# Attention and mixture of experts in one kernel: the first slot's split divided over two attention units, and the weights' scales taken with their first split

## The chip, the cores and the metric

One core of one Trainium2 chip. The metric is the device time in microseconds of one execution. The kernel before takes 730.81 us (median of 3 runs, 727.73 to 730.84).

## What is computed

For 8 batches of 8 heads, 576 positions and 64 channels, attention is computed twice: on queries, keys and values pooled by four, and locally, within three positions to either side. The sum is the input of a mixture of 8 experts with one expert per token.

```python
out_d = sm_attn(q_d, k_d, v_d)                       # pooled by 4
out_up = np.repeat(out_d, factor, axis=2)
mask = np.abs(pos[:, None] - pos[None, :]) < factor
out_local = np.matmul(attn, v)                       # softmax under the mask
x = (out_up + out_local) -> [N=4608, 512]
...
logits = xn @ en.T / tau
expert_idx = np.argmax(logits, axis=1)
for e in range(E):
    h = np.maximum(x[mask] @ w1[e], 0.0)             # 512 -> 1024
    out[mask] = gate_w[mask, None] * (h @ w2[e])     # 1024 -> 512
```

## The kernel before

**Attention.** There are 32 units: 8 batches of four head pairs. `attention` (a generator) runs a software pipeline over `i` from −2 to 32. In one iteration unit `i+2` has its queries and keys transposed (`qk_T`, PE L378; four ACT copies to `kq`, L379) and pooled on POOL (L392, and the values' `pool_v` L401); unit `i+1` its scores (L407, L412, pooled L434), maxima and exponentials (DVE L423 and L424, L443; ACT L425, L454), row sums, `inv`, and the normalised weights `an` (L472) and `ad` (L477) on DVE; unit `i` the transposes of its weights (PE L485 and L496; ACT copies `aT` L488 and `adT` L498) and the products with the values (L505, L521; ACT `od` L511, DVE `xT` L523); unit `i-1` the transposes to rows of `x` and the experts' logits (L536, L539; ACT `xr` L543, DVE L546; `ls` L548 and L550). The order of instructions on every engine is that in which the program writes them, and each engine runs its own in order; seven PSUM banks go round among the matmuls' results.

**What is placed between.** The generator stops at marks, and the caller puts other work there: `yield i, 0` in the middle of an iteration, `yield i, 3` in front of the rows' copies in iteration 30, `yield i, 1` at the end.

```python
for at in steps:
    if at is None:
        break
    if at in EARLY:
        next(early)
    i, end = at
    if end and i >= 1 and i % NHP in heavy:
        heavy = next(w0, ())
```

`early_slots` makes the lists of the first three expert slots from the tokens that are already there: `ege` and `efull`, then `parts` (L694), which PE multiplies (L702), then the ids (L706 to L732) and on POOL three gathers by them from `xd` in DRAM (L1126), then slot 0's measure (`x_size`: ACT's square L1144, DVE's logits and scale L1145, L79 to L81) and its split into two halves of 16 bits (`x_split`: ACT L1153, DVE L1156, and a transpose by DMA, L1158), then slot 1's. `first_weights` prepares the first expert's weights in four pieces each of `w1` and `w2`: squares and sums on ACT (L859), a total over the partitions with a matmul (L868), the scale `wscl` from it on DVE (L869 to L878), then for each piece the high half on ACT (`w1h`, `w2h`, L882) and the low half on DVE (L887), put off until behind unit `i+1`'s pooled maxima. What a step yields says at which `i % 4` the next may come: `FREE` at any, `LIGHT` at 0, 2, 3, `HEAVY` at 0, 3. Its last two steps issue the loads of the second expert's `w1`, four of 512 KB on SP's queue. When the attention's loop is over, the slots follow, 41 in all, with the matmuls of L1205 to L1207 (`x` by `w1`) and L1228 to L1230 (by `w2`), each product in three parts of 16-bit halves. `warm_up(n)` issues n matmuls of 512 columns whose result nobody reads (L337).

Of the kernel before, what the change touches and what calls it, by code (L numbers as in the profile page):

```python
# [9 lines left out]
F16 = mybir.dt.float16  # L10
BF16 = mybir.dt.bfloat16
I32 = mybir.dt.int32
AF = mybir.ActivationFunctionType
ALU = mybir.AluOpType
# [6 lines left out]
N, DM, E, FF = B * S, H * D, 8, 1024  # L21
# [20 lines left out]
LW = TB + TR  # L42
XS, HS, EB = 3, 10, 127
FIRST = 3
EARLY = ((28, 0), (28, 1), (29, 0), (30, 3), (31, 0), (31, 1))
MASKED = -1.0e30
QS = 0.125 / 16

# [3 lines left out]
class Kern:  # L52
# [128 lines left out]
    def attention(self, ctx):  # L181
# [56 lines left out]
        for i in range(-2, n + 1):  # L238
            a, c, d, e = i + 2, i + 1, i, i - 1
            if a < n:  # L240
                st[a] = {"u": a, "j": a % 2, "vw": self.vw[a // 2 % 2], **half[a // 2]}
                self.qk_T(st[a])
            if a == n:
                self.warm_up(2)
            if 0 <= c < n:
                self.scores(st[c])
                if not c:
                    self.warm_up(3)
            if a < n:
                self.pooled(st[a])  # L250
                for u in range(a if a > 1 else 0, a + 1 if a else 0):
                    self.pooled_v(st[u])
                if a % 2:
                    load_v(a // 2 + 1)
            if i in (0, 2):
                next(clists)
            if 0 <= d < n:
                self.weights_T(st[d])
            if 0 <= c < n:
                self.scores_d(st[c])  # L260
                self.exps(st[c])
                self.peaks_d(st[c])
                while self.later:
                    self.later.pop(0)()
                if c == n - 1:
                    self.exps_d(st[c])
            if 0 <= d < n:
                self.weights_dT(st[d])
                if not d:
                    self.warm_up(7)  # L270
            if 0 <= c < n - 1:
                self.exps_d(st[c])
            yield i, 0
            if mid:
                mid.pop()()
            for _ in range(2 if BEARLY * NHP <= i < (BEARLY + 1) * NHP else 1):
                if tail and i < n - 1:
                    tail.pop(0)()
            self.shared, parts = self.bank(), None
            if 0 <= e < n:  # L280
                b, hp = units[e]
                if hp == 0:
                    xr[b] = (self.rt.tile([TB, NTB, XW], F32, name="xr", bufs=2),
                             self.rt.tile([128, LP], F32, name="ls")[:, :LW])
                parts = self.rows(st.pop(e), hp, *xr[b])
            if 0 <= d < n:
                self.values_d(st[d])
            if c == n - 1:
                self.sums_l(st[c])
                self.inverses(st[c])  # L290
                self.normalise_l(st[c])
                self.normalise_d(st[c])
                yield i, 3
            if 0 <= c < n - 1:
                self.sums_l(st[c])
            if parts:
                parts[1]()
            if 0 <= d < n:
                self.out_d(st[d])
            if 0 <= c < n - 1:  # L300
                self.inverses(st[c])
                self.normalise_l(st[c])
            if 0 <= d < n:
                self.values(st[d])
            if parts:
                parts[0]()
                if hp == NHP - 1:
                    while tail and b >= BEARLY:
                        tail.pop(0)()
                    tail += self.place(b, *xr.pop(b), mid)  # L310
                    if b == B - 2:
                        tail.pop(0)()
            if 0 <= c < n - 1:
                self.normalise_d(st[c])
            if i == n - 1:
                tail.pop(0)()
            if i == -1:
                next(crows)
                nc.vector.memset(self.lg, 0.5)
                nc.vector.memset(self.oh, 0.0)  # L320
            if a >= 0 and a % 2 == 1:
                load(a // 2 + 2)
                if a == 1:
                    load_w(1)
            if d >= 0 and d % 2 == 1:
                load_w(d // 2 + 2)
            yield i, 1
# [384 lines left out]
    def early_slots(self):  # L712

        nc, v = self.nc, self.nc.vector
        c = self.cp
        self.ids = c.tile([128, NEARLY + NSLOT], I32, name="ids")
        full = c.tile([128, 1], F32, name="efull")
        lim = c.tile([128, NEARLY], F32, name="elim")
        for i in range(NEARLY):
            v.memset(lim[:, i:i + 1], float(SLOT * (i + 1)))  # L720
        ge = c.tile([128, NEARLY], F32, name="ege")

        v.tensor_scalar(out=ge, in0=lim, scalar1=self.base[:, 0:1], scalar2=None, op0=ALU.is_le)
        v.reduce_sum(out=full[:, 0:1], in_=ge, axis=AX.X)
        v.tensor_scalar(out=ge, in0=ge, scalar1=-float(PADID), scalar2=float(PADID), op0=ALU.mult, op1=ALU.add)
        self.nearly = full[:, 0:1]
        yield
        parts = self.id_parts(c, self.pb[:, :BEARLY].rearrange("p b t -> p (b t)"), BEARLY, NEARLY)
        yield
        idf = c.tile([128, NEARLY], F32, name="idf")  # L730
        self.ids_of(c, parts, BEARLY * NTB, NEARLY, idf)
        v.tensor_tensor(out=self.ids[:, :NEARLY], in0=idf, in1=ge, op=ALU.max)  # L732
        for q in range(NEARLY):
            self.gather(q)
        yield
        self.x_size(0)
        self.norms(0)
        self.x_split(0)
        yield
        self.x_size(1)  # L740
        yield
        self.x_split(1)
        self.begun = [self.mm1_half(0, 0, 0, 2)]
        yield
# [155 lines left out]
    def first_weights(self):  # L900
# [35 lines left out]
        square(0, 0, 1)  # L936
        yield LIGHT
        square(0, 2, 3)
        yield FREE
        self.total(slice(0, 1))  # L940
        self.scales(slice(0, 1))
        self.keep_scale()
        yield HEAVY
        split(0, 0)
        yield HEAVY
        split(0, 1)
# [5 lines left out]
        square(1, 0, 1)  # L952
        yield LIGHT
        square(1, 2, 3)
        yield FREE
        self.total(slice(1, 2))
        self.scales(slice(1, 2))
        yield HEAVY
        split(1, 0)
        yield HEAVY  # L960
        split(1, 1)
# [1 line left out]
        split(1, 2)  # L963
        yield HEAVY
        split(1, 3)
        self.out_scale()
        for i in range(2):
            yield FREE
            for j in range(2):
# [165 lines left out]
        self.x_split(q, other)  # L1135

    def x_size(self, q):
        nc, s = self.nc, self.sl[q]
        xg = s["xg"]
        v = nc.vector  # L1140
        ss = s["ss"] = self.mx.tile([SLOT, 1], F32, name="ss", bufs=4)
        sc = s["sc"] = self.mx.tile([SLOT, 1], F32, name="sc", bufs=4)
        lg = s["lg"] = self.mx.tile([SLOT, E], F32, name="lg", bufs=4)
        nc.scalar.activation(out=self.jk[:, :DM], in_=xg[:, :DM], func=AF.Square, accum_out=ss)  # L1144
        v.tensor_copy(out=lg, in_=xg[:, DM:])  # L1145
        self.pow2(self.mx, ss, sc)

    def x_split(self, q, other=None):
        nc, s = self.nc, self.sl[q]
        xs = s.pop("xg")[:, :DM]  # L1150
        v, sc = nc.vector, s["sc"]
        x2 = self.mx.tile([SLOT, 2, DM], F16, name="x2")
        nc.scalar.activation(out=x2[:, 0], in_=xs, func=AF.Copy, scale=sc)  # L1153
        if other is not None:
            self.logits(other)
        v.scalar_tensor_tensor(out=x2[:, 1], in0=xs, scalar=sc, in1=x2[:, 0], op0=ALU.mult, op1=ALU.subtract)  # L1156
        xT = s["xT"] = self.mx.tile([128, 2, self.KC, SLOT], F16, name="xT2", bufs=3)
        nc.sync.dma_start_transpose(out=xT.rearrange("p t c s -> p (t c) s"), in_=x2.rearrange("p a f -> p (a f)"))  # L1158

# [86 lines left out]
    def run(self):  # L1246
# [9 lines left out]
        with ExitStack() as actx:  # L1256
            w0 = self.first_weights()
            steps = self.attention(actx)
            early, heavy = self.early_slots(), FREE
# [3 lines that stand above are left out]
                if at in EARLY:  # L1263
                    next(early)
                i, end = at
                if end and i >= 1 and i % NHP in heavy:
                    heavy = next(w0, ())

            ps = self.begun
            self.x_size(2)  # L1270
            self.mm1_half(0, 0, 2, 3, ps[0])
            next(steps)
            self.mm1_half(0, 0, 3, 4, ps[0])
            ps.append(self.mm1_half(0, 1, 0, 2))
            next(steps)
            next(steps)
            for _ in steps:
                pass
# [96 lines left out]
```

## Time and profile before

| | |
|---|---|
| median of 3 runs | 730.81 us (727.73 to 730.84) |
| the profiled execution | 730.06 us, span 728.1 us |
| mean granted clock of TensorE, share of full | 0.983 |
| PE busy | 698.2 us, 96% |
| DVE, ACT, POOL busy | 464.4, 466.7, 403.7 us |
| DMA | 117.82 MB, mean 162 GB/s |

Times of rows are microseconds from the span's start. The duration of a merged row (x4) runs from the first instruction's start to the last one's end; idle time stands in brackets, with what was seen to end it. Attention takes the first 270 us or so of the span, the slots the rest. Unit `i`'s transposes (L485) begin at 87.90 for `i` = 9 and at 262.56 for `i` = 31, the last.

### The profile page before, as it was taken

Reading aid. Unit: us, or ns where it says so; the run is one execution under the profiler, and the core shown is the slowest. Engines: PE = TensorE matmul, PEld = TensorE weight load, DVE = VectorE, ACT = ScalarE, POOL = GpSimd, SP = SyncE. Lnnn points to the kernel's source line nnn. Section 1 sums busy time; section 2 is a strip of 40 time slices with the busy share of each in tenths; the row PEclk is TensorE's granted clock in tenths of the full one; section 3 lists DMA queues with packets and bytes.
Section 4 is the critical chain, followed back from the end, with each engine's and each line's share of the span. In section 5 each row is a group of like instructions: output and inputs, shape, how many; then the busy total and the mean of one; then the engine's idle time right before and its main releaser. Section 6 shows DMA issues by size and latency. Waiting matters only on the chain. (4 is left out here: it accounts for less than half of the span.)

```text
span 728.1 us, 27458 instructions
## 1 busy us (share of the span) xinstructions
PE 698.2 (96%) x10501; PEld 527.0 (72%) x10501; DVE 464.4 (64%) x1395; ACT 466.7 (64%) x1095; POOL 403.7 (55%) x800
## 2 busy tenths in 40 slices
PE   8998999999999989999999999999999999999993
PEld 5787787787878667677767767766776776777671
DVE  6777788797898958757446466564754375456420
ACT  4787877888877654556746658576673367357520
POOL 8554646765776916547543554556465535535421
PEclk9999999999999879999999999999999999999997
DMA  8999887999968357344826566386673346348300
GB/s 192 196 239 255 177 225 161 257 246 196 236 154 226 86 185 212 89 101 165 184 78 200 167 185 187 103 242 113 181 171 87 90 165 177 90 126 214 60 31 20
DMA packets 191238, 117.82 MB, mean 162 GB/s; under 512 B 162898, under 2 KB 162898, under 8 KB 191072
## 3 DMA queue, kind: packets, MB, share of 16 engines
q1 hardware_dynamic: 183264, 94.61, 53.1%
q0 software_dynamic: 6560, 19.03, 8.4%
q10 hardware_dynamic: 1248, 2.11, 1.0%
q8 instruction: 85, 1.39, 0.8%
q14 instruction: 81, 0.66, 0.3%
HBM read 213.12 MB, written 20.33 MB: 321 GB/s over the span
## 5 line engine op out<-in xcount | busy, mean ns | idle before, releaser
L1207 PE MATMUL bank<-xT,w1l 128*128 128x128 f16 x1312 | 223.3, 219 | 2.9 <-DVE w1l L887 1.4
L1206 PE MATMUL bank<-xT,w1h 128*128 128x128 f16 x1312 | 223.5, 219 | 0.4 <-issue 0.3
L1205 PE MATMUL bank<-xT,w1h 128*128 128x128 f16 x1312 | 223.6, 219 | 0.0
L1205 PEld LDWEIGHTS <-w1h 128*128 128x128 f16 x1312 | 128.6, 98 | 7.0 <-issue 2.4
L1207 PEld LDWEIGHTS <-w1l 128*128 128x128 f16 x1312 | 128.6, 98 | 5.0 <-DVE w1l L887 2.6
L1206 PEld LDWEIGHTS <-w1h 128*128 128x128 f16 x1312 | 128.6, 98 | 4.1 <-issue 0.5
L1230 PE MATMUL bank<-w2h,hT 128*128 128x512 f16 x328 | 124.3, 379 | 0.0
L1229 PE MATMUL bank<-w2l,hT 128*128 128x512 f16 x328 | 124.2, 379 | 0.0
L1228 PE MATMUL bank<-w2h,hT 128*128 128x512 f16 x328 | 124.2, 379 | 0.0
L1242 POOL DMA_INDIRECT out_dram<-o,ids x40 | 51.0, 1274 | 111.8 <-ACTq L1042 74.3
L1217 DVE SCALAR_TENSOR_TENSOR hT<-bank,hT 128x512 f16<-128x512 f32 x82 | 54.9, 686 | 44.3 <-ACT hT L1216 19.7
L1216 ACT ACTIVATE hT<-bank 128x512 f16<-128x512 f32 x82 | 46.6, 587 | 51.0 <-PE bank L868 33.1
L392 POOL TENSOR_TENSOR pool_kq<-kq 128x288 f32<-128x288 f32 x62 | 40.2, 670 | 56.4 <-ACT kq L379 54.7
L1156 DVE SCALAR_TENSOR_TENSOR x<-xg,sc,x 128x512 f16<-128x512 f32 x41 | 30.8, 751 | 60.1 <-ACT x L1153 52.9
L859 ACT ACTIVATE junk<-st 128x1024 bf16<-128x1024 f32 (+1 forms) x30 | 67.5, 2248 | 2.1 <-POOL at L618 1.6
L1126 POOL DMA_INDIRECT xg<-xd,ids x41 | 44.4, 1083 | 38.7 <-POOLq L1048 17.2
L401 POOL TENSOR_TENSOR pool_v<-ld_v 72x256 f32<-72x256 f32 x64 | 54.6, 873 | 18.7 <-DMA ld_v<-in_v_dram 17.1
L1230 PEld LDWEIGHTS <-hT 128*128 128x128 f16 x328 | 32.0, 98 | 38.7
L1228 PEld LDWEIGHTS <-hT 128*128 128x128 f16 x328 | 32.0, 98 | 33.8
L1229 PEld LDWEIGHTS <-hT 128*128 128x128 f16 x328 | 32.0, 98 | 33.8
L1174 ACT ACTIVATE lg<-lg,lmx 128x8 f32<-128x8 f32 x41 | 12.3, 300 | 66.8 <-DVE lmx L1172 65.6
L488 ACT ACTIVATE aT<-bank 70x384 f32<-70x384 f32 x96 | 40.1, 486 | 20.9 <-PE bank L485 20.8
(238 smaller groups left out, 1519.3 us busy)
## 6 DMA issues: line engine op xcount, KB each, us to landing
st<-in_moe_w_dram SPq DMA_DIRECT2D x148, 1024.0 KB
ld_k<-in_k_dram SPq DMA_DIRECT2D x64, 144.0 KB
ld_q<-in_q_dram SPq DMA_DIRECT2D x64, 144.0 KB
ld_v<-in_v_dram SPq DMA_DIRECT2D x16, 576.0 KB
vw<-in_v_dram SPq DMA_DIRECT2D x16, 576.0 KB
xd<-xr SPq DMA_DIRECT2D x8, 1040.0 KB
st<-in_moe_w_dram SPq DMA_DIRECT2D x12, 512.0 KB
st<-in_moe_w_dram ACTq DMA_DIRECT2D x4, 512.0 KB
```

What stands on the lines that cost most here:

```text
L401: g.tensor_tensor(out=t6[:, h], in0=vr[:, :, 0:2 * D], in1=vr[:, :, 2 * D:], op=ALU.add)
L859: self.nc.scalar.activation(out=junk, in_=src, func=AF.Square, accum_out=acc)
L1126: nc.gpsimd.indirect_dma_start(out=xg, out_offset=None, in_=self.xd[:n], in_offset=bass.IndirectOffsetOnAxis(ap=self.ids[:, q:q + 1], axis=0),
L1205: nc.tensor.matmul(out=o, lhsT=self.w1h[:, k, f], rhs=xT[:, 0, k], start=(k == 0), stop=False)
L1206: nc.tensor.matmul(out=o, lhsT=self.w1h[:, k, f], rhs=xT[:, 1, k], start=False, stop=False)
L1207: nc.tensor.matmul(out=o, lhsT=self.w1l[:, k, f], rhs=xT[:, 0, k], start=False, stop=(k == self.KC - 1))
L1216: nc.scalar.activation(out=h[:, 0], in_=ps, func=AF.Relu)
L1217: nc.vector.scalar_tensor_tensor(out=h[:, 1], in0=ps, scalar=0.0, in1=h[:, 0], op0=ALU.max, op1=ALU.subtract)
L1228: nc.tensor.matmul(out=ps, lhsT=hh, rhs=self.w2h[:, j, :], start=(j == 0), stop=False)
L1229: nc.tensor.matmul(out=ps, lhsT=hh, rhs=self.w2l[:, j, :], start=False, stop=False)
L1230: nc.tensor.matmul(out=ps, lhsT=hl, rhs=self.w2h[:, j, :], start=False, stop=(j == self.FC - 1))
L1242: nc.gpsimd.indirect_dma_start(out=self.out, out_offset=bass.IndirectOffsetOnAxis(ap=self.ids[:, q:q + 1], axis=0), in_=o, in_offset=None, ...
```

## The change

The table `EARLY`, which says at which marks `early_slots` goes on, has nine entries instead of six. The first (`ege`) moves from iteration 28 to 27 and `parts` to the middle of iteration 28. Slot 0's measure and split are cut into four steps: the square at a new mark `(30, 4)`, ahead of `weights_T`; logits and scale at a new mark `(30, 5)`, behind unit 31's maxima and exponentials; the high half at `(30, 0)`; the low half and the transpose at `(30, 3)`, which moves from in front of the rows' copies to behind unit 30's values. The two warm-up matmuls of iteration 30 go. In `first_weights`, total and scales come in the same step as the first split, for `w1` and for `w2`, and the outputs' scale with the latter; such a step, now `HEAVY`, comes where the split alone came an iteration or more later.

```diff
-EARLY = ((28, 0), (28, 1), (29, 0), (30, 3), (31, 0), (31, 1))
+EARLY = ((27, 0), (28, 0), (29, 0), (30, 4), (30, 5), (30, 0), (30, 3), (31, 0), (31, 1))
...
-            if a == n:
-                self.warm_up(2)
             if 0 <= c < n:
                 self.scores(st[c])
...
+            if c == n - 1:
+                yield i, 4
             if 0 <= d < n:
                 self.weights_T(st[d])
             if 0 <= c < n:
                 self.scores_d(st[c])
                 self.exps(st[c])
+                if c == n - 1:
+                    yield i, 5
                 self.peaks_d(st[c])
...
                 self.normalise_d(st[c])
-                yield i, 3
...
             if 0 <= c < n - 1:
                 self.normalise_d(st[c])
+            if c == n - 1:
+                yield i, 3
...
-        self.x_size(0)
+        self.x_square(0)
+        yield
+        self.x_scale(0)
         self.norms(0)
-        self.x_split(0)
+        yield
+        self.x_high(0)
+        yield
+        self.x_low(0)
         yield
...
-        yield FREE
+        yield HEAVY
         self.total(slice(0, 1))
         self.scales(slice(0, 1))
         self.keep_scale()
-        yield HEAVY
         split(0, 0)
...
-        yield FREE
+        yield HEAVY
         self.total(slice(1, 2))
         self.scales(slice(1, 2))
-        yield HEAVY
+        self.out_scale()
         split(1, 0)
...
         split(1, 3)
-        self.out_scale()
...
     def x_size(self, q):
+        self.x_square(q)
+        self.x_scale(q)
...
     def x_split(self, q, other=None):
...
+        self.x_high(q)
         if other is not None:
             self.logits(other)
...
+        self.x_low(q)
...
-                if end and i >= 1 and i % NHP in heavy:
+                if end == 1 and i >= 1 and i % NHP in heavy:
                     heavy = next(w0, ())
```

`x_square`, `x_scale`, `x_high` and `x_low` hold the lines that `x_size` and `x_split` held: the square into `ss`; the copy of the logits `lg` and the scale `sc`; ACT's copy with that scale; DVE's rest and the transpose.

The weights' steps come so: `w1`'s splits at the end of iterations 8, 11, 12, 15 (before: 11, 12, 15, 16), the squares of `w2` in 16 and 18 (18, 19), its total in 19 (20), its splits in 19, 20, 23, 24 (23, 24, 27, 28). On SP's queue the first load of a `w2` piece moves ahead of the second store of `xd`, and the four loads of the second expert's `w1` stand together ahead of the last `ld_v`; before, two stood behind the store of `xd` in iteration 29 and two behind slot 0's transpose. POOL's order is unchanged. In the rows that follow, the lines of the changed program are some 3 to 19 higher.

ACT at the end of iteration 8 and the start of iteration 9, before (`kq_111` and `kq_107` are the two buffers of `kq`, `st_749` is the staged weights):

```order
L511 ACTIVATE od<-bank 128x144
L543 ACTIVATE xr<-bank 128x4x128
L379 ACTIVATE kq_111<-bank 128x288 x4
L488 ACTIVATE aT<-bank 70x384 x3
L425 ACTIVATE a<-a 128x342
L498 ACTIVATE adT<-bank 72x288 x2
L454 ACTIVATE ad,sums_110<-bank,md 72x144 x4
```

and now:

```order
L514 ACTIVATE od<-bank 128x144
L546 ACTIVATE xr<-bank 128x4x128
L890 ACTIVATE w1h<-st_749,wscl 128x2x512
L382 ACTIVATE kq_111<-bank 128x288 x4
L491 ACTIVATE aT<-bank 70x384 x3
L428 ACTIVATE a<-a 128x342
L501 ACTIVATE adT<-bank 72x288 x2
L457 ACTIVATE ad,sums_110<-bank,md 72x144 x4
```

The split `w1h`, which waits for `wscl`, stands between `xr` and the copies of `kq`; it stood there in iteration 11 before.

ACT from the end of iteration 29 to the end of iteration 30, before (`junk,ss<-xg` is slot 0's square, `x_6006` its high half):

```order
L511 ACTIVATE od<-bank 128x144
L543 ACTIVATE xr<-bank 128x4x128
L488 ACTIVATE aT<-bank 70x384 x3
L425 ACTIVATE a<-a 128x342
L454 ACTIVATE ad,sums_114<-bank,md 72x144 x4
L498 ACTIVATE adT<-bank 72x288 x2
L1144 ACTIVATE junk,ss<-xg 128x512
L1153 ACTIVATE x_6006<-xg,sc 128x512
L511 ACTIVATE od<-bank 128x144
L543 ACTIVATE xr<-bank 128x4x128
```

and now:

```order
L514 ACTIVATE od<-bank 128x144
L546 ACTIVATE xr<-bank 128x4x128
L1151 ACTIVATE junk,ss<-xg 128x512
L491 ACTIVATE aT<-bank 70x384 x3
L428 ACTIVATE a<-a 128x342
L457 ACTIVATE ad,sums_114<-bank,md 72x144 x4
L501 ACTIVATE adT<-bank 72x288 x2
L1169 ACTIVATE x_5984<-xg,sc 128x512
L514 ACTIVATE od<-bank 128x144
L546 ACTIVATE xr<-bank 128x4x128
```

The square moved from behind unit 30's `adT`, where the high half stood too, to ahead of unit 30's `aT`; the high half stayed.

DVE in iteration 30, before (`sc` and `pw_h` are the scale's steps, `x_6006<-xg,sc` the low half of slot 0, `ls` the last rows' copy):

```order
L465 RECIPROCAL inv<-inv 128x13
L472 TENSOR_TENSOR an_113<-a,inv 64x9x38 x2
L477 TENSOR_TENSOR ad<-ad,inv 72x576
L1145 COPY lg<-xg 128x8
L79 TENSOR_SCALAR pw_h<-ss 128x1
L80 TENSOR_SCALAR pw_h<-pw_h 128x1
L81 TENSOR_SCALAR sc<-pw_h 128x1
L1156 SCALAR_TENSOR_TENSOR x_6006<-xg,sc,x_6006 128x512
L546 COPY xr<-bank 128x128
L548 TENSOR_TENSOR ls<-ls,bank 128x192
L523 TENSOR_TENSOR xT_108<-bank,od 128x320
L523 TENSOR_TENSOR xT_108<-bank,od 128x256
```

and now:

```order
L81 TENSOR_SCALAR sc<-pw_h 128x1
L446 TENSOR_REDUCE md<-bank 72x2 x2
L462 TENSOR_REDUCE sums_114<-a 128x9
L467 TENSOR_SCALAR inv<-sums_114 128x13
L468 RECIPROCAL inv<-inv 128x13
L475 TENSOR_TENSOR an_113<-a,inv 64x9x38 x2
L480 TENSOR_TENSOR ad<-ad,inv 72x576
L549 COPY xr<-bank 128x128
L551 TENSOR_TENSOR ls<-ls,bank 128x192
L526 TENSOR_TENSOR xT_108<-bank,od 128x320
L526 TENSOR_TENSOR xT_108<-bank,od 128x256
L1174 SCALAR_TENSOR_TENSOR x_5984<-xg,sc,x_5984 128x512
```

The scale moved ahead of `md`, the maxima of unit 31, and the low half from ahead of `xr` and `ls` to behind `xT`.

## Rows read from the trace of the kernel before

**Rows 1.** The page's first part: busy us (share) and instructions of engines.

```profile
PE 698.2 (96%) x10501; PEld 527.0 (72%) x10501; DVE 464.4 (64%) x1395; ACT 466.7 (64%) x1095; POOL 403.7 (55%) x800
```

**Rows 2.** PE's timeline, 244–275 us: start, duration, instruction, count, [idle before <-releaser].

```profile
247.76 0.90 PE L702 MATMUL bank<-parts,at 128*128 128x6 bf16 x30 [0.94 <-DVE a L424]
...
256.58 1.18 PE L485 MATMUL bank<-ident,an 128*70 128x128 f32 x9
...
260.82 0.76 PE L505 MATMUL bank<-adT,vd 72*64 72x144 f32 x8 [0.71 <-ACT adT L498]
...
265.78 0.98 PE L496 MATMUL bank<-ident,ad 72*72 72x72 f32 x8 [2.05 <-ACT od L511]
...
271.78 0.27 PE L1205 MATMUL bank<-xT,w1h 128*128 128x128 f16 x1
```

**Rows 3.** Windows: length, busy PE PEld DVE ACT POOL, clock, DMA share, GB/s.

```profile
136.00:144.00 8.00, 7.99 (x176) 6.48 (x175) 5.56 (x14) 7.02 (x22) 7.76 (x13) 1.00 0.97 217
218.00:223.00 5.00, 4.43 (x91) 3.42 (x93) 3.87 (x10) 3.25 (x9) 3.25 (x5) 0.66 1.03 331
249.60:256.50 6.90, 6.63 (x128) 4.76 (x127) 6.06 (x24) 1.50 (x7) 4.61 (x5) 0.51 0.67 210
266.70:273.60 6.90, 6.90 (x82) 5.84 (x81) 3.20 (x16) 3.23 (x9) 0.12 (x1) 0.51 0.57 176
```

**Rows 4.** Instructions of tile w1h: ns min/median/max, first and last start.

```profile
L882 ACT ACTIVATE w1h<-st,wscl x32: 1131/1134/1151, 108.5 to 648.2; 128x1024 f16<-128x1024 f32 x32
```

**Rows 5.** ACT's timeline, 84–93 us: copies of kq at iteration 8's end.

```profile
85.65 1.32 ACT L379 ACTIVATE kq<-bank 128x288 f32<-128x288 f32 x4
```

**Rows 6.** DVE's timeline in 84–93 us: ad and the scale of the weights.

```profile
87.08 0.74 DVE L477 TENSOR_TENSOR ad<-ad,inv 72x576 f32<-72x576 f32 x1
...
88.18 0.14 DVE L878 TENSOR_SCALAR wscl<-wk 128x1 int32<-128x1 int32 x1
```

**Rows 7.** PE's timeline in 84–93 us: the transposes of unit 9's weights.

```profile
87.90 1.18 PE L485 MATMUL bank<-ident,an 128*70 128x128 f32 x9
```

**Rows 8.** DVE's timeline in 171–181 us: ad in iteration 19.

```profile
172.56 0.74 DVE L477 TENSOR_TENSOR ad<-ad,inv 72x576 f32<-72x576 f32 x1
```

**Rows 9.** PE's timeline in 169–183 us: L485 beside squares, and a wait.

```profile
172.75 1.51 PE L485 MATMUL bank<-ident,an 128*70 128x128 f32 x9
...
180.25 0.30 PE L407 MATMUL bank<-mask,identb 128*128 128x342 bf16 x1 [0.46 <-DVE xT L523]
```

**Rows 10.** DVE's timeline in 240–268 us.

```profile
248.35 1.27 DVE L887 SCALAR_TENSOR_TENSOR w2l<-st,wscl,w2h 128x1024 f16<-128x1024 f32 x1
...
253.38 1.03 DVE L472 TENSOR_TENSOR an<-a,inv 64x342 f32<-64x342 f32 x2
...
264.11 0.75 DVE L1156 SCALAR_TENSOR_TENSOR x<-xg,sc,x 128x512 f16<-128x512 f32 x1 [0.79 <-ACT x L1153]
```

**Rows 11.** POOL's timeline in 228–268 us.

```profile
230.31 1.42 POOL L401 TENSOR_TENSOR pool_v<-ld_v 72x256 f32<-72x256 f32 x2
...
247.26 2.95 POOL L401 TENSOR_TENSOR pool_v<-ld_v 72x256 f32<-72x256 f32 x2
...
251.31 1.27 POOL L1126 DMA_INDIRECT xg<-xd,ids  x1 [0.30 <-DVE lmx L588]
```

**Rows 12.** DMA queues, 255–257 us: packets, MB, share; q0 is the gathers'.

```profile
q0 software_dynamic: 75, 0.26, 39.1%
```

**Rows 13.** ACT's timeline in 242–268 us.

```profile
257.20 1.24 ACT L488 ACTIVATE aT<-bank 70x384 f32<-70x384 f32 x3 [3.33 <-PE bank L485]
...
260.94 0.64 ACT L1144 ACTIVATE junk<-xg 128x512 bf16<-128x512 f32 x1
```

**Rows 14.** DMA queues in 266.5–267.5 us.

```profile
q1 hardware_dynamic: 810, 0.20, 106.4%
```

**Rows 15.** Timeline of SP's queue in 228–268 us.

```profile
231.76 0.30 SPq L354 DMA_DIRECT2D ld_v<-in_v_dram  x1
```

**Rows 16.** PE's timeline in 131–138 us: a gap in iteration 15.

```profile
136.01 0.27 PE L485 MATMUL bank<-ident,an 128*70 128x128 f32 x1 [1.19 <-issue]
```

More of the change, by code (lines that the diff above doesn't have):

```diff
@@ L1137, in x_size, with x_square, x_scale, x_high @@
     def x_size(self, q):
+        self.x_square(q)
+        self.x_scale(q)
+    def x_square(self, q):
         nc, s = self.nc, self.sl[q]
         xg = s["xg"]
-        v = nc.vector
         ss = s["ss"] = self.mx.tile([SLOT, 1], F32, name="ss", bufs=4)
+        nc.scalar.activation(out=self.jk[:, :DM], in_=xg[:, :DM], func=AF.Square, accum_out=ss)
+    def x_scale(self, q):
+        s = self.sl[q]
         sc = s["sc"] = self.mx.tile([SLOT, 1], F32, name="sc", bufs=4)
         lg = s["lg"] = self.mx.tile([SLOT, E], F32, name="lg", bufs=4)
-        nc.scalar.activation(out=self.jk[:, :DM], in_=xg[:, :DM], func=AF.Square, accum_out=ss)
-        v.tensor_copy(out=lg, in_=xg[:, DM:])
-        self.pow2(self.mx, ss, sc)
+        self.nc.vector.tensor_copy(out=lg, in_=s["xg"][:, DM:])
+        self.pow2(self.mx, s["ss"], sc)
     def x_split(self, q, other=None):
[L1149 to L1153, printed above, removed]
+        self.x_high(q)
         if other is not None:
             self.logits(other)
-        v.scalar_tensor_tensor(out=x2[:, 1], in0=xs, scalar=sc, in1=x2[:, 0], op0=ALU.mult, op1=ALU.subtract)
+        self.x_low(q)
+    def x_high(self, q):
+        s = self.sl[q]
+        x2 = s["x2"] = self.mx.tile([SLOT, 2, DM], F16, name="x2")
+        self.nc.scalar.activation(out=x2[:, 0], in_=s["xg"][:, :DM], func=AF.Copy, scale=s["sc"])
+    def x_low(self, q):
+        nc, s = self.nc, self.sl[q]
+        xs, x2 = s.pop("xg")[:, :DM], s.pop("x2")
+        nc.vector.scalar_tensor_tensor(out=x2[:, 1], in0=xs, scalar=s["sc"], in1=x2[:, 0], op0=ALU.mult,
+                                       op1=ALU.subtract)
         xT = s["xT"] = self.mx.tile([128, 2, self.KC, SLOT], F16, name="xT2", bufs=3)
```

## Prediction, made before the changed kernel ran

> **What bounds the kernel now.** I first read the page's busy times: TensorE (PE) works for 96% of the span [rows 1], so a change is worth what it does to PE's start times and to its clock. Next I followed PE's timeline, attention unit by attention unit, looking for idle time in brackets, and for what the engine named there was doing. The hand-over from attention to the expert slots is where it shows: L702 starts after 0.94 us of idle time, L505 waits 0.71 us, L496 waits 2.05 us, and only at 271.78 does the first slot's first matmul (L1205) start [rows 2]. Last I read the windows for the granted clock: 0.51 in 249.6–256.5 and in 266.7–273.6, 0.66 over 218–223, against 1.00 in 136–144 [rows 3]. [...] A stretch of 6.9 us costs up to half of it, 3.4, where PE is what the others wait for; the one in 218–223 costs (1 − 0.66) × 5 = 1.7.
>
> **The early weights: a loss.** Total, scales and split of the first piece now come in one step. At the end of iteration 8 ScalarE (ACT) gets `w1h`, 1.13 us [rows 4], directly ahead of the four `kq` copies that began at 85.65 [rows 5]. It needs `wscl`, which VectorE (DVE) makes only behind `ad`: done at 88.18 + 0.14 = 88.32 [rows 6]. So ACT stands still with `kq` queued behind it: `w1h` from 88.37, `kq` from about 89.45, 3.8 us later. `kq` empties PSUM banks that the transposes of L485 need: six of the nine, which began at 87.90 [rows 7], run until about 88.65, and the last three wait for the first `kq` copy, done near 89.45 + 0.35 = 89.8. PE idles 1.2 us, and with the copies behind I take **+1.3** (bounds: 0.6, if one more bank is free, and 2.4, if the later copies hold PE up too).
>
> Iteration 19 is the same with `w2h`. `ad` starts at 172.56 [rows 8]; in iteration 8 it started at 87.08, 1.24 us before `wscl` was done [rows 6], so `wscl` comes at 173.80 and `kq` near 174.9. L485 there began at 172.75, took 1.51 us and ended at 174.26 [rows 9]; now its last third waits for 174.9 + 0.35 and ends near 175.6, 1.35 later, with one idle piece of some 1.8 us in it. Part comes back, because PE then waited 0.46 us for DVE at 180.25 [rows 9] and DVE need not be late: **+0.9** (0.5 to 1.4). In iteration 16 two squares stand where a split stood; L485 beside squares took 1.51, beside none 1.18 [rows 7, 9]: **+0.3** (0 to 0.5). The other steps of the weights trade a split for a split, or a square for a square: nothing, the same work stands in the same place of another unit. The first `w2` piece, loaded earlier, puts 512 KB ahead of loads on SP's queue; those are issued a pair of units before they are used, which hides it: nothing, at most 1.5 us (512 KB at the 331 GB/s of rows 3) if not. Together **+2.5** (1.1 to 4.3).
>
> **The late part: a gain.** The splits `w2l` and `w2h` leave iterations 28 and 29 (as the loop counts where DVE does them), and the lists of slot 0 move ahead. Three things follow.
>
> First, `parts` are made ahead of unit 30's row sums, so L702 doesn't wait for them: about 246.7 instead of 247.76. With 1.27 us of `w2l` at 248.35 [rows 10] gone from between, DVE reaches the ids some 1.9 us sooner (1.1 from L702, the rest until L702's result is the later one), and so also `an`, at 251.5 instead of 253.38 [rows 10]. L485 of unit 30, at 256.58 before [rows 2] at the end of a stretch at half clock and of two warm-ups, now starts as soon as `an` is there: near 252.5.
>
> Second, GpSimd (POOL): two `pool_v` took 2.95 us at 247.26, beside `w2l`, and 1.42 at 230.31, without it [rows 11]. With 1.5 us less there, the first gather starts near 249.7 instead of 251.31 [rows 11]. Its 0.26 MB passed in 255 to 257 [rows 12], so it had landed by 257.0, 5.7 us after its start. I keep 5.4, since two weight loads no longer share that time: 255.1. ACT's square (0.64 and a small read, 0.85 together) now stands ahead of `aT` of unit 30, so this landing counts: `aT` at 256.0 against 257.20 [rows 13]. L505, 3.6 us behind `aT` as before, comes near 259.5 instead of 260.82 [rows 2]. Between 252.5 and 259.5 PE waits some 4 us in pieces: a new wait, of ACT for the gather, takes the place of lost clock.
>
> Third, the split of slot 0. DVE did the scale and the low half `x`, 0.75 us at 264.11 [rows 10], ahead of `ls`; ACT's `od` waited for `ls`, and L496 for `od`, 2.05 us [rows 2]. Now the scale is made before unit 31's peaks, ACT's high half follows `adT`, and the low half stands behind `xT`. With all of it 1.35 us sooner, the 1.5 us of scale, wait and `x` out of the way, L496 starts near 263.0 instead of 265.78. From there to L1205 it was 6.0 us, 5.1 of it at the 0.51 of rows 3; at full clock 0.9 + 2.6 and some weight loads, I take 4.1: L1205 at 267.1. The low half is done near 264.1, and its transpose moved its packets until 267.5 [rows 14], 2.6 us behind the end of `x`: 266.7. That is just in time, and it is what is late next if DVE slips.
>
> L1205 at 271.78 was followed by 1.8 us at half clock, which cost 0.9, so it stood like 272.65: 5.5 us gained at full clock. I take off 0.5 for one short stretch at half clock in iteration 30, where PE waits anyway: **−5.0**. Bounds: −6.5 (gather at its soonest), −2.1 (6.9 us at half clock from 263 on, 3.4 off).
>
> Four loads of 512 KB go ahead of the `ld_v` issued at 231.76 [rows 15]. At 331 GB/s they take 6.3 us; the tile comes near 239.5 to 240, about when `pool_v` of unit 30 wants it. If it is late, POOL's list work and the gathers, which are queued behind, are late by as much; cover is the 1.5 us that `pool_v` saves. Nothing, up to 1.5.
>
> Sum: +2.5 − 5.0 = **−2.5** against the profiled execution's 730.06, which is 0.75 under the median of 730.81. Against the median: **728.3**.
>
> [...] The gather's packets passed only in 255 to 257 [rows 12], four microseconds after its start, while SP's queue had a store and two loads to move. [...] By the row the gather lands at 255.1, as summed. [...]
>
> **The rivals.**
> 1. [...] Chance 0.15.
> 2. *The clock stays up.* The loss in 218–223 may not return once all before it is shifted by 2.5 us (1.7), nor any in iteration 30 (0.5): −4.7, **726.1**. Against it: the waits in the late part are shorter, not gone. Chance 0.13.
> 3. *The gather lands no sooner*, at 257.0, so the change doesn't bring what it is moved for. Square, `aT` and what follows are 1.9 later than I count, though the split is still out of DVE's way before `ls`: late gain 2.5 to 3, sum about 0, **730.8**. Chance 0.20.
> 4. *The clock falls at the new waits*, the slower side. Place: PE's idle pieces of 1.2 us in iteration 8 and 1.8 in iteration 19. Price: 3.4 each, by the 249.6–256.5 row, which followed a gap of just 0.94; 1.7 each by the 218–223 row. It decides once both fall for long: −2.5 + 6.8 = +4.3, **735.1**; both short, +0.9, 731.7. Against it: the 1.19 us gap at 136.01 [rows 16] was followed by 1.00 [rows 3]. Chance 0.13.
>
> The forecast keeps 0.39.
>
> **How the numbers follow.** About 0.5%, 3.65 us, is what a measurement of this kernel can tell from no change, so 727.2 to 734.5 counts as the same. Rivals 1 and 2 lie below, by 0.5 and 1 us, so most of their 0.28 counts, 0.20, and the forecast with its lower bounds gives 0.10: faster 0.30. Rival 4 with long stretches, 0.07, and the upper bounds of the third and of the early terms, 0.05: slower 0.12. The rest, 0.58, is the same. The range goes from rival 2 less 1.1 (the early terms nearer to their lower bound), 725.0, to 733.5: rival 3 with the early terms at 4.3 is 732.6, and rival 4 with one short and one long stretch 733.4.
>
> **What would show it.** Right: ACT idle before `w1h` at 88 and before `w2h` at 174, with L485 broken in two there; no idle time at L702; gather 0 near 249.7; the square ahead of `aT` at 255; L496 near 263; L1205 near 267. Wrong: PE not idle in iterations 8 and 19 (no early loss: 725.8); a stretch below 1.00 behind either; the gather's packets not before 257; L1205 waiting for the transpose and not for PE, which would say that DVE ends the hand-over.

## The result, and the profile after

The changed kernel takes 737.26 us (median of 13 runs, 731.69 to 740.93); the kernel before, in 13 runs beside them, 730.81. The ratio is 1.0083 with an interval of 1.0055 to 1.0112: about 6 us slower, outside the range of the prediction (725.0 to 733.5) and on the other side. The profiled execution took 734.77, its span is 732.8. All ratios leave out the executions that lie over 1.5% above the fastest of their kernel.

The page's first part, the counterpart of [rows 1]: PE works no longer than before, so the time went into waits.

```profile
PE 696.9 (95%) x10499; PEld 525.7 (72%) x10499; DVE 464.0 (63%) x1395; ACT 466.5 (64%) x1095; POOL 402.4 (55%) x800
```

Windows of the clock, as in [rows 3]: one stretch of 3.4 us near 200 and one of 13.6 in the hand-over; at the first slot's first matmul, 277.24, the clock is full again (1.00 in 276–280).

```profile
199.00:204.00 5.00, 5.00 (x102) 4.05 (x101) 2.04 (x4) 2.54 (x7) 4.92 (x8) 0.66 1.11 240
...
254.30:267.90 13.60, 12.37 (x157) 9.28 (x158) 9.59 (x31) 3.99 (x12) 10.13 (x20) 0.50 0.46 149
268.00:276.00 8.00, 7.60 (x132) 5.97 (x132) 5.29 (x18) 5.54 (x20) 0.00 (x0) 1.00 0.10 19
```

PE's timeline in 84–97 and 174–180 us, against [rows 7], and ACT's, against [rows 5]: the transposes of unit 9 are broken in two, 1.11 us apart, because `kq` stands behind `w1h`, and `w1h` waits 2.86 us for `wscl`.

```profile
88.12 0.85 PE L488 MATMUL bank<-ident,an 128*70 128x128 f32 x6
90.08 0.52 PE L488 MATMUL bank<-ident,an 128*70 128x128 f32 x3 [1.11 <-ACT kq L382]
...
177.21 0.52 PE L488 MATMUL bank<-ident,an 128*70 128x128 f32 x3 [1.11 <-ACT kq L382]
```

```profile
88.58 1.15 ACT L890 ACTIVATE w1h<-st,wscl 128x1024 f16<-128x1024 f32 x1 [2.86 <-DVE wscl L886]
89.63 1.30 ACT L382 ACTIVATE kq<-bank 128x288 f32<-128x288 f32 x4
```

This is as forecast, to 0.2 us: `kq` at 89.63 (89.45), PE idle 1.11 us (1.2). In iteration 19, where some 1.8 us were forecast, PE is idle 1.11 us too, ahead of 177.21. Then, in iteration 22, something that the prediction does not name, in PE's timeline; the clock window at 199–204 above follows it.

```profile
198.56 0.33 PE L524 MATMUL bank<-aT,vw 70*64 70x64 f32 x3 [1.66 <-issue]
```

In the hand-over, POOL's timeline, against [rows 11], and that of SP's queue, against [rows 15]:

```profile
243.51 0.67 POOL L396 TENSOR_TENSOR kqd<-pool_kq 128x288 f32<-128x288 f32 x1
249.29 1.42 POOL L404 TENSOR_TENSOR pool_v<-ld_v 72x256 f32<-72x256 f32 x2 [5.11 <-DMA ld_v<-in_v_dram]
...
251.49 2.91 POOL L673 TENSOR_SCALAR at<-iota,pm 128x128 bf16<-128x128 f32 x5
...
258.88 1.27 POOL L1132 DMA_INDIRECT xg<-xd,ids  x1 [0.30 <-DVE oh L595]
```

```profile
235.80 3.11 SPq L997 DMA_DIRECT2D st<-in_moe_w_dram  x4
239.01 0.43 SPq L357 DMA_DIRECT2D ld_v<-in_v_dram  x1
...
256.51 0.39 SPq L568 DMA_DIRECT2D xd<-xr  x1
```

POOL is done with `kqd` at 244.18 and waits 5.11 us for `ld_v`. That load was issued at 239.01, behind the four loads of 512 KB, which SP issued from 235.80, when it was through with `vw`. So POOL's last five `at` start at 251.49 and the gather at 258.88. PE's timeline, against [rows 2]:

```profile
253.01 1.04 PE L705 MATMUL bank<-parts,at 128*128 128x6 bf16 x28 [0.23 <-issue]
254.45 0.19 PE L705 MATMUL bank<-parts,at 128*128 128x6 bf16 x1 [0.40 <-POOL at L673]
...
263.87 2.13 PE L488 MATMUL bank<-ident,an 128*70 128x128 f32 x9
...
269.58 0.76 PE L508 MATMUL bank<-adT,vd 72*64 72x144 f32 x8 [0.39 <-ACT adT L501]
...
272.50 0.98 PE L499 MATMUL bank<-ident,ad 72*72 72x72 f32 x8
```

```profile
277.24 0.23 PE L1224 MATMUL bank<-xT,w1h 128*128 128x128 f16 x1 [0.75 <-DMA xT<-x]
```

L705 (L702 before) now waits for POOL's `at`, but for 0.23 and 0.40 us only (the first is named "issue"). What else the late list costs is not read from one wait here: behind it PE has few gaps, and runs at half clock from 254.3 to 267.9 (0.50 above). That the stretch follows from the late list is not shown; what the loads' place costs in all, the experiments measure. From unit 28's L485 (236.25 before, 241.81 now) to the first slot's first matmul it was 35.5 us, and it is 35.4: the hand-over, which was to gain 5 us, gained nothing, and before it the attention had lost 5.6. ACT's timeline, against [rows 13]: the square waits 2.21 us for the gather, and `aT` then for PE at half clock, so that the gather is not what ends last here. The first slot's first matmul, at 277.24, waits 0.75 us for its own transpose `xT`, which the prediction had among the signs of being wrong.

```profile
262.62 0.63 ACT L1151 ACTIVATE junk<-xg 128x512 bf16<-128x512 f32 x1 [2.21 <-DMA xg<-xd,ids]
...
264.81 1.07 ACT L491 ACTIVATE aT<-bank 70x384 f32<-70x384 f32 x2 [1.48 <-PE bank L488]
```

### The profile page after: what moved, and what is told of

Same layout as the page of the kernel before. It is cut to its first block, busy times and chain, and to the rows that moved or that the text cites. A ratio compares the mean times of both kernels' runs of the same rounds, so it can differ in the third digit from the quotient of the medians.

```text
span 732.8 us, 27459 instructions
## 1 busy us (share of the span) xinstructions
PE 696.9 (95%) x10499; PEld 525.7 (72%) x10499; DVE 464.0 (63%) x1395; ACT 466.5 (64%) x1095; POOL 402.4 (55%) x800
## 3 DMA queue, kind: packets, MB, share of 16 engines
q8 instruction: 85, 1.39, 0.8%
## 5 line engine op out<-in xcount | busy, mean ns | idle before, releaser
L404 POOL TENSOR_TENSOR pool_v<-ld_v 72x256 f32<-72x256 f32 x64 | 51.4, 823 | 32.4 <-DMA ld_v<-in_v_dram 32.3
L1247 PEld LDWEIGHTS <-hT 128*128 128x128 f16 x328 | 32.0, 98 | 33.8
L1248 PEld LDWEIGHTS <-hT 128*128 128x128 f16 x328 | 32.0, 97 | 33.8
```

Of the source, the lines that this page charges most:

```text
L404: g.tensor_tensor(out=t6[:, h], in0=vr[:, :, 0:2 * D], in1=vr[:, :, 2 * D:], op=ALU.add)
L1247: nc.tensor.matmul(out=ps, lhsT=hh, rhs=self.w2h[:, j, :], start=(j == 0), stop=False)
L1248: nc.tensor.matmul(out=ps, lhsT=hh, rhs=self.w2l[:, j, :], start=False, stop=False)
```

## The experiments

The theory after these traces ("loads"): the four early loads of the second expert's weights make `ld_v`, and through POOL's queue the lists and the gather, late, and undo what the late part gains. The rivals: ACT's wait for `wscl` with the clock behind it; the square ahead of `aT`, which makes ACT wait for the gather; PE's own pauses that the profile names "issue". The next table holds all runs. The third column is the time from unit 9's L485 to unit 23's in the one profile of each (it holds iterations 8 to 22), the fourth that from unit 28's L485 to the first slot's L1205, both from PE's timeline; an asterisk marks a third column in which the granted clock fell. The last two columns tell of one execution each and don't add up to the ratios: that of e11 was the longest of its thirteen, those of e1, e6 and e13 were among the longest of theirs, and those of e8 and e9 among the shortest.

| run | ratio to before, 95% interval | units 9 to 23, us | hand-over, us |
|---|---|---|---|
| before | | 108.2 | 35.5 |
| the change | 1.0083 (1.0055–1.0112) | 113.6* | 35.4 |
| e9, the change again | 1.0098 (1.0065–1.0131) | 110.9 | 35.2 |
| e1, loads held to 29, 30 | 1.0020 (0.9994–1.0046) | 118.0* | 32.6 |
| e2, late half alone | 1.0034 (1.0008–1.0059) | 108.1 | 35.7 |
| e3, early half alone | 1.0141 (1.0114–1.0168) | 111.6 | 40.9 |
| e4, e1 and halves behind `kq` | 1.0017 (0.9988–1.0047) | 109.4 | 33.2 |
| e5, e4 with loads at 27, 28 | 0.9984 (0.9951–1.0017) | 112.5* | 32.8 |
| e10, e5 again | 1.0010 (0.9975–1.0045) | 109.8 | 33.0 |
| e6, the change with loads at 27, 28 | 1.0021 (0.9986–1.0055) | 116.6* | 31.2 |
| e7, e3 with loads at 27, 28 | 1.0013 (0.9970–1.0056) | 112.1 | 33.8 |
| e8, before with 64 small matmuls | 1.0012 (0.9972–1.0052) | 110.3* | 32.8 |
| e11, e5, store later | 0.9978 (0.9949–1.0007) | 115.8* | 33.6 |
| e12, e5, square back | 1.0021 (0.9990–1.0051) | 110.9 | 33.2 |
| e13, e11 again | 0.9981 (0.9948–1.0015) | 115.8* | 30.6 |
| e14, e13 with halves ahead of `kq` | 1.0013 (0.9981–1.0044) | 113.5* | 31.1 |

### Where the loads stand: e1, e3, e6, e7

e1 is the change with the loads held back to the ends of iterations 29 and 30:

```diff
         for i in range(2):
-            yield FREE
+            yield LAST
...
+LAST = (0, 1, 2, 3, 29)
...
-                if end == 1 and i >= 1 and i % NHP in heavy:
+                if end == 1 and i >= 1 and i % NHP in heavy and i >= (heavy + (1,) * 5)[4]:
```

> The change, but the four 512 KB loads of the second expert's w1 are held until the ends of iterations 29 and 30, as before the change. Theory 'loads': in the profile of the change POOL waited 5.1 us for ld_v behind those loads, and with that gather 0 started at 258.9; held back, gather 0 starts 5 us or more sooner relative to unit 29's transposes and the time falls by 3 to 5 us against the change, to 1.002 to 1.005 of before. Theory 'ACT waits for wscl': the loss is made in iterations 8 and 19 and the loads are covered: the ratio stays at 1.008.

It came out as the theory has it: 4.6 us under the change (0.0063 × 730.8), with some 3 us of uncertainty. In e1's POOL timeline `pool_v` doesn't wait for its load, and the gather starts 12.4 us after unit 28's L485 (245.69), where it took 15.1 before and 17.1 in the change:

```profile
248.03 1.80 POOL L405 TENSOR_TENSOR pool_v<-ld_v 72x256 f32<-72x256 f32 x2
...
258.05 1.27 POOL L1133 DMA_INDIRECT xg<-xd,ids  x1 [0.35 <-DVE lmx L592]
```

But ACT's timeline of e1 shows the price of the place that they now have, beside the gather:

```profile
265.43 0.63 ACT L1152 ACTIVATE junk<-xg 128x512 bf16<-128x512 f32 x1 [4.88 <-DMA xg<-xd,ids]
```

The gather landed 7.35 us after its start, and ACT waited 4.88 for it.

e3 is the kernel before with the weights' steps of the change, so the early half alone:

```diff
-        yield FREE
+        yield HEAVY
         self.total(slice(0, 1))
         self.scales(slice(0, 1))
         self.keep_scale()
-        yield HEAVY
         split(0, 0)
```

(and the same for `w2`, with `out_scale`).

> The early half alone: the kernel before with the new steps of the weights (total and scales in the step of the first split, so loads of the second expert ahead of ld_v too). Theory 'loads': early loss 2.5 plus the late ld_v, POOL's lists and gathers late by 3 to 5 us, in front of the old hand-over: ratio 1.006 to 1.010. Theory 'ACT waits' alone: 2.5 us less the gain of w2's splits out of iterations 27 and 28 (about 1.5): 1.001 to 1.003.

Slower than the "loads" theory had it. POOL's and PE's timelines of e3: with the old lists the wait for `ld_v` is 10.32 us. L702 stands still for 4.35 us (named "issue"), and its last matmuls then come one by one with POOL's `at`, which went on only at 254.09.

```profile
251.91 1.40 POOL L401 TENSOR_TENSOR pool_v<-ld_v 72x256 f32<-72x256 f32 x2 [10.32 <-DMA ld_v<-in_v_dram]
```

```profile
254.57 0.94 PE L702 MATMUL bank<-parts,at 128*128 128x6 bf16 x27 [4.35 <-issue]
...
257.06 0.18 PE L702 MATMUL bank<-parts,at 128*128 128x6 bf16 x1 [0.39 <-POOL at L670]
```

e6 and e7 are the change and e3 with the loads behind the last `ld_v` and `vw` (the lines of e1, with one number changed):

```diff
-LAST = (0, 1, 2, 3, 29)
+LAST = (0, 1, 2, 3, 27)
```

> The change as it is, with only the four loads moved to the ends of iterations 27 and 28. Theory 'place of the loads': 5 us or more under the change, 1.000 to 1.002. Against e5 it tells what ACT's wait for wscl costs: by the prediction 2.2 us (1.3 and 0.9), by the traces so far, with the clock, 2 to 4.

> As e3_weights_only (the early half alone, with the old late part), with the four loads at the ends of iterations 27 and 28. Theory 'place of the loads': at least 6 us under e3's 1.0141, so at or under 1.006; what is left is the early loss of 2.5 us less what the missing w2 splits in iterations 27 and 28 give: 1.000 to 1.004. If the ratio stays over 1.010, the early steps themselves cost what e3 lost.

SP's queue and POOL in e6:

```profile
240.44 0.30 SPq L358 DMA_DIRECT2D ld_v<-in_v_dram  x1
242.99 3.38 SPq L368 DMA_DIRECT2D vw<-in_v_dram  x3
246.42 3.31 SPq L998 DMA_DIRECT2D st<-in_moe_w_dram  x4
```

```profile
247.96 1.82 POOL L405 TENSOR_TENSOR pool_v<-ld_v 72x256 f32<-72x256 f32 x2
...
258.19 1.27 POOL L1133 DMA_INDIRECT xg<-xd,ids  x1 [0.55 <-DVE lg L583]
```

`ld_v` goes first and nobody waits for it. e7 is 9.4 us under e3, e6 4.5 under the change as first measured and 5.6 under e9. Three pairs of kernels that differ in the loads' place alone (e1, e6, e7) agree: that place is what cost the change most of its 6 us. What is left, 1.0 to 1.5 us over before, cannot be told from none.

### The late half alone: e2

e2 takes the new `EARLY`, the divided split and no warm-up, with the weights' steps of before.

> The late half of the change alone: the new EARLY table, the split x_ steps and no warm-up, but the weights' steps (total one step ahead of the first split) and loads at their places of before; w2's last splits are then again in iterations 27 and 28. Theory 'loads' and theory 'ACT waits': the hand-over gains, 2 to 4 us (less than the 5 of the prediction, since w2l is back on DVE beside pool_v): ratio 0.994 to 0.997. Theory 'the square ahead of aT costs': ACT waits for the gather and nothing is gained: 1.000 or above.

The rival was right here: 2.5 us slower. PE's timeline of e2:

```profile
256.63 1.15 PE L488 MATMUL bank<-ident,an 128*70 128x128 f32 x9 [2.17 <-DVE an L475]
...
262.06 0.70 PE L499 MATMUL bank<-ident,ad 72*72 72x72 f32 x4 [2.65 <-ACT aT L491]
```

With `w2`'s splits still in iterations 27 and 28 the gather starts 14.9 us after unit 28's L485 and lands at 260.9; the square in front of `aT` passes this wait on to PE, 2.65 us ahead of L499. Does the late half pay with those splits out of the way? e3 and the change differ by the late half alone, and so do e7 and e6. Where the loads make `ld_v` late, it gains 4.2 us (1.0141 to 1.0083). With the loads moved, e7 and e6 cannot be told apart (1.0013 and 1.0021, with some 4 us of uncertainty).

### ACT's wait for the scale: e4, e5, e10, e14, e9

In e4 (from e1) and e5 (from e6) the first piece's high half goes to the next iteration:

```diff
-            self.split_h(src, which, p)
+            if p:
+                self.split_h(src, which, p)
+            else:
+                self.later.append(lambda: self.split_h(src, which, p))
```

> As e1_loads_held, and the high half of each weight's first piece is put behind unit i+1's exponentials in the next iteration, where wscl has long been made, so that kq does not queue behind a waiting ACT. Theory 'ACT waits': 1.5 to 2 us less than e1_loads_held (no idle piece of PE in L485's transposes in iterations 8 and 19). Theory 'loads' alone, with the early waits costing nothing: as e1_loads_held.

> As e4_held_behind_kq, but the four loads go to the ends of iterations 27 and 28: on SP's queue behind the last ld_v and vw, ahead of iteration 29's store of xd. In the runs so far gather 0 landed 6.7 to 7.5 us after its start where two of the loads stood beside it and 3.7 to 3.8 where none did, and POOL waited 5.1 us for ld_v where they stood ahead of it. Theory 'place of the loads': both are avoided, gather 0 lands 3 to 4 us after its start, the idle time ahead of L496 in iteration 30 (3.0 in e4) falls to 1 or less, and the time is 2 to 3 us under e4: ratio 0.997 to 0.999. Theory 'clock': the hand-over's lost clock is set by PE's waits there in any case: as e4, 1.001 to 1.003.

> The change itself once more, beside the variants on one chip. All theories: about 1.008 of before (1.0055 to 1.0112 so far). If it comes out under 1.004, much of what was put down to the loads was the chip of the first measurement.

> e5_loads27_behind_kq once more (loads behind the last ld_v and vw, first pieces' high halves behind kq). Theory 'place of the loads': 4 to 6 us under the change beside it, 0.996 to 1.001 of before.

PE's timeline of e4 has unit 9's transposes in one piece again:

```profile
89.07 1.18 PE L489 MATMUL bank<-ident,an 128*70 128x128 f32 x9
```

The three pairs differ by 0.2 us (e1, e4), 2.7 (e6, e5) and, below, 2.3 (e14, e13): 1.7 in the mean, each with some 3 us of uncertainty. In the profiles without a fall of the clock, units 9 to 23 take 110.9 to 112.1 with the wait (e3, e7, e9), 109.4 to 110.9 without (e4, e10, e12), 108.1 and 108.2 with the old steps (before, e2): 3.4 us for the early half, 1.5 of them for this wait. e5's gather landed 6.1 us after its start, not 3 to 4: that part of its expectation failed. The change measured again (e9) confirms the result.

### What the gather waits for: e11, e12, e13, e14

In e11 (from e5) the store of batch 6's rows to `xd`, which the first gathers don't read, moves behind slot 0's transpose:

```diff
-            if b < B - 1:
+            if b < B - 2:
                 save(nc.sync)
+            elif b == B - 2:
+                self.held = save
...
         self.x_low(0)
+        self.held(self.nc.sync)
```

> As e5, with the store of batch 6's rows to xd (1.17 MB on SP's queue, issued just before the gathers, which don't read those rows) put behind slot 0's transpose. In all runs so far gather 0 landed 1.2 to 2.4 us after that store had, whenever it started. Theory 'the gather passes behind the store': gather 0 lands 3 to 4 us after its start instead of 6.1, ACT's wait for it ahead of the square goes, and the time falls by 0 to 2 us (where PE is at half clock there, nothing). Theory 'the gather's own time': 6 us as in e5.

> e11_store_later once more: loads behind the last ld_v and vw, first pieces' high halves behind kq, the store of batch 6 behind slot 0's transpose. Theory 'place of the transfers': 0.995 to 1.000 of before again, 6 us or more under the change.

POOL and ACT in e13:

```profile
258.85 1.27 POOL L1139 DMA_INDIRECT xg<-xd,ids  x1 [0.60 <-DVE lg L583]
```

```profile
262.48 0.63 ACT L1158 ACTIVATE junk<-xg 128x512 bf16<-128x512 f32 x1 [0.60 <-DMA xg<-xd,ids]
```

The gather lands 3.6 us after its start and ACT waits 0.60 us, in e11 not at all. (The 1.2 to 2.4 us between the store's landing and the gather's, which e11's expectation gives for all runs, is not right for e5, e6 and e7: there both landed within 0.2 us.) Both measurements lie 1.5 us under before, with intervals that just take in no change; on the chip of e9, the median of e11 is 6.6 us under that of e9. This is the best version found, clearly faster than the change and not clearly faster than before.

> As e13, but the first pieces' high halves stand ahead of kq again, where ACT waits for wscl, as in the change. Theory 'ACT waits': 1.5 to 3 us over e13 (0.002 to 0.004; e5 and e6 differed by 2.7 us, e1 and e4 by 0.2). Theory 'the wait is given back': the same as e13.

> As e5, with slot 0's square back behind unit 30's adT, scale, high and low half all at the mark behind unit 30's xT. Theory 'the divided split gains' (the prediction's): mm1 waits for slot 0's transpose 2 us longer, +1 to +2 us against e5. Theory 'the square ahead of aT costs': ACT doesn't wait for the gather, aT of unit 30 comes up to 2 us sooner: -1 to 0 us against e5.

```diff
-EARLY = ((27, 0), (28, 0), (29, 0), (30, 4), (30, 5), (30, 0), (30, 3), (31, 0), (31, 1))
+EARLY = ((27, 0), (28, 0), (29, 0), (30, 0), (30, 3), (31, 0), (31, 1))
...
         self.x_square(0)
         yield
         self.x_scale(0)
         self.norms(0)
-        yield
         self.x_high(0)
-        yield
         self.x_low(0)
```

e12 lies 0.8 us over e10 on the same chip, within what can be told: inconclusive. Whether the square's place gains is open, the more so as e12 moves the scale and the split with it.

### PE's pauses: e8

```diff
-        self.warm_up(8)
+        self.warm_up(8, 64)
...
+        for _ in range(small):
+            nc.tensor.matmul(out=ps[:, :8], lhsT=z[:, :128], rhs=z[:, :8], start=True, stop=True)
```

> The kernel before, with 64 matmuls of 8 columns (128 instructions of PE with their weight loads) behind the warm-up at the start, where PE waits for the first loads in any case. It tests what the waits named 'issue' in PE's timeline are. [...] Theory 'data': the pauses stay at the same instructions of the same units.

Before, a pause named "issue" stands in unit 6's L496 (1.75 us, to 66.39) and one in unit 15's L485 (1.19 us, to 136.01 [rows 16]). In e8 both groups of matmuls are whole, L496's (L498 here) from 64.20 and L485's from 132.11, and other instructions are held up:

```profile
132.11 1.18 PE L487 MATMUL bank<-ident,an 128*70 128x128 f32 x9
```

```profile
68.93 0.66 PE L380 MATMUL bank<-ident,ld_k 96*128 96x96 f32 x6 [1.26 <-issue]
```

```profile
162.11 0.57 PE L523 MATMUL bank<-aT,vw 70*64 70x64 f32 x12 [1.93 <-issue]
```

So the two pauses did not stay with the data of their units: with 128 instructions of PE more in front, it is other instructions that are held up, by 1.26 and 1.93 us. What holds them up the run does not show. No change of the time can be told. And e8's hand-over, which has the code of before, had a full clock in its profile and took 32.8 us instead of 35.5:

```profile
236.00:270.00 34.00, 28.11 (x592) 21.90 (x591) 27.82 (x82) 21.25 (x68) 21.86 (x33) 1.00 0.51 139
```

## Why the prediction was wrong

Forecast were −2.5 us, measured +6.1. Two terms of the sum failed: the four loads, put at nothing, cost 4.5 to 5.6, and the late part, put at −5.0, brought some 1 to 2.

**The early weights (+2.5): right in kind, small in size.** The wait of ACT, its place and PE's idle piece came as worked out; profiles without a fall of the clock give 3.4 us instead of 2.5, inside the bounds of 1.1 to 4.3. The wait for `wscl` was put at 2.2 and measured 1.5 to 1.7, so that some 1.8 us lie elsewhere in the early half, where the prediction had 0.3.

**The four loads ("Nothing, up to 1.5"): the first step that failed.** Their place measured 4.5 to 5.6 us in the change, and 9.4 with the old late part. The loads' own time was right: in the change their 2 MB pass in 238.1–244.5, 6.4 us where 6.3 were forecast. Wrong was what stands on either side. They start 4.2 us after unit 27's L485 (233.88) instead of 2.7: SP issued `ld_k`, `ld_q` and `vw` ahead of them until 235.76, and the loads' packets, of 4 KB, start at 238.1, where those of 256 B ahead of them run out (the last at 239.0). And `ld_v` behind them got only 1.4 to 1.9 us for its own passage, its bytes at the rate of the big loads. In the trace of before, with none of these loads ahead of it, it took 5.7 us from issue (231.76) to landing (237.49). In the change its packets pass in 244.0–248.4, beside those of the `vw` issued behind it, while the queues move 189 GB/s instead of the 352 of the loads' stretch; it lands at 249.2, 4.7 us behind the loads and 15.3 after unit 27's L485 instead of the 10.5 to 11 of the prediction. Windows of the change, columns as in [rows 3]:

```profile
238.10:244.40 6.30, 5.97 (x149) 4.91 (x144) 6.03 (x18) 4.04 (x13) 5.04 (x9) 1.00 1.00 352
244.40:249.20 4.80, 3.90 (x69) 3.21 (x68) 4.15 (x14) 3.21 (x14) 0.00 (x0) 1.00 1.04 189
```

The cover that I named, 1.5 us from `pool_v`, was there and too small by 5.1.

**The lists and the gather (−5.0 together): right in place, wrong in size.** The gather was forecast 13.5 us after unit 28's L485 and came at 12.4 to 14.5 in the versions with the new late part and the loads moved. L1205 was forecast at 30.9 after it and came at 30.6 to 31.2 in e6, e13 and e14, in the others at 32.6 to 33.6. The gather's landing was wrong: 5.4 us was taken from [rows 12], where the trace's landing event of the gather of before stands at 258.05, 6.7 us after its start; 7.2 to 7.5 came with two loads beside it (e1, e2, e4), 6.1 with the store alone (e5, e6), 3.6 without either (e13), 3.7 in the change, where the store had gone 2.4 us ahead.

By the times, little of the 5 us is left. e6 has the whole change with the loads out of the way and stands 1.5 us over before; with 2.5 (forecast) to 3.4 us (measured) for the early half, the late part brought some 1 to 2. e6 against e7 shows no gain of the late half at all, within some 4 us. Two things bear on it, and neither is shown to be the cause. I took off 0.5 us for half clock in the hand-over, and the profile of the change has 13.6 us at 0.50 there; in e5 the same 36 matmuls of L525 take 2.13 us at 256.71 and 1.22 at 266.79. And I counted the hand-over of before as 35.5 us with both its stretches at half clock, as if these belonged to the code. e8 has the same code there, only shifted by 128 instructions of PE, and took 32.8 at full clock (1.00 in 236–270). It is one execution of each, and that of e8 one of its shortest, so which of the two is usual is open. Against 32.8, the versions with the loads moved would gain up to 2.2 us in the hand-over or lose up to 0.8, and they lose 2 to 3.4 early.

**The rivals.** The second (the clock stays up) did not hold: the stretch in 218–223 is gone from the profile of the change (1.00 in 218–230), but one of 3.4 us at 0.50 stands at 199.7 and one of 13.6 us in the hand-over. The third (the gather lands no sooner) came near in what it saw, for a cause it didn't have: the gather landed at 262.5, 20.7 us after unit 28's L485, where before had 21.8 and the forecast 18.9, because it started late. The fourth (the clock falls at the new waits) did not hold in the profile of the change: the 1.11 us pieces in iterations 8 and 19 were followed by a full clock there (1.00 in 89–104 and in 177–186); in the third column of e6, whose steps there are those of the change, it fell. In the change it fell in iteration 22, behind the pause of 1.66 us. The first has 0.15 of the chances, and the bound of −6.5 counts on a gather at its soonest; no run shows one that lands more than 0.2 us ahead of the store. With the store beside it the gather took 6.1 us (e5, e6), with the store out of the way 3.6 (e13). Its first packet starts 4.2 us after its start in the trace of before, at 255.53, while the store's packets pass in 252.0–256.0, and 2.2 us after it in the change, at 261.10, 0.2 us behind the end of the store's last.

Not settled: how much of the spread between executions of one kernel (727.73 to 734.54 for before in the first measurement, without its longest) is the clock and how much the pauses, since each kernel has one or two profiles.

## What to carry to other kernels

When a change makes some steps come sooner, follow what they issue on the DMA queue to the end of that queue. Here four loads that nobody needed yet stood ahead of one that POOL waited for: their 2 MB passed in 6.4 us, `ld_v` landed 4.7 us behind them, POOL waited 5.11 us for it, and the gather, behind that on POOL, started 17.1 us after unit 28's L485 instead of 15.1 before and 12.4 with the loads held back (e1). Count from where the queue is free (here 238.1, where the first load was issued at 235.80), and give the load that is waited for its own time from issue to landing as the trace has it (here 5.7 us), not its bytes at another load's rate (1.4 to 1.9). And don't book a stretch at low clock as part of the code on the word of one execution (here 35.5 us with two stretches at 0.51, and 32.8 at 1.00 in e8): take a second profile, and one of the same code shifted a little, and see if it is there again.

## What the hardware showed that was not expected

Some of PE's pauses that the profile names "issue" end shortly behind a packet of the queue that it names "instruction", q8: 85 packets, 1.39 MB, in the pages of before and of the change, beside some 21,000 matmuls and weight loads each. In the change no packet of that queue started between 185.8 and 196.2; from 15 to 272 us one starts every 6.1 us on average. From 192 on SP's transfers kept the DMA engines busy, mostly to 90% or more; PE stood still from 196.90 to 198.56 and went on 1.4 us after the packet of 196.2 was through. The DMA queues in 196–197.3 us:

```profile
q1 hardware_dynamic: 535, 0.41, 100.7%
q8 instruction: 1, 0.02, 4.6%
```

In the traces of before and of the change this holds for all nine pauses of the attention of 0.5 us or more that are named "issue": each ends 1.3 to 1.6 us behind the end of such a packet. Before they end at 66.39, 112.86 and 136.01 (1.75, 0.90 and 1.19 us), in the change at 66.61, 104.82, 137.55, 166.81, 198.56 and 247.57 (1.20, 0.67, 1.38, 0.51, 1.66 and 0.91 us). Two stand at nearly the same place in the count of PE's matmuls in both traces: behind the 1,222nd, and behind the 2,731st before and the 2,730th in the change. The others stand in one of the two traces only.

Pauses of that name stand in the matmuls by `parts` as well: 4.35 us in e3 (L702) and 1.06 in e5 (L706). What the pauses cost a version in all, and whether the loads have a part in them, was not measured: the traces show only that the times stand beside each other.
